# Another sequence of turns for a fused GLA-and-MLP kernel on one core

## The chip, the core and the metric

The kernel runs on one core of a Trainium2 chip. Five engines work side by side, each through its own instructions in its own fixed order: TensorE (PE; its weight loads are listed as PEld), VectorE (DVE), ScalarE (ACT), GpSimd (POOL) and SyncE (SP), which here issues nearly all DMA transfers. An engine that waits for a semaphore holds up everything that stands behind that instruction in its own order. The metric is the device time of one execution in microseconds (us), the median over several runs.

## The reference

Four batches, eight heads, 768 positions, head size 48. First a gated linear attention, a recurrence over the positions, then a layer norm, two matrix products with a relu between them, and a residual:

```python
for t in range(S):
    state = alpha[:, :, t, :, None] * state + np.einsum('bhd,bhe->bhde', k[:, :, t], v[:, :, t])
    y[:, :, t] = np.einsum('bhd,bhde->bhe', q[:, :, t], state)
...
xn = (x - mu) / np.sqrt(var + 1e-06) * g_ln
ch = np.maximum(xn @ w_ch1, 0.0) @ w_ch2
return (x + ch).astype(np.float32)
```

x is y with the heads side by side (4 x 768 x 384); w_ch1 is 384 x 1536 and w_ch2 is 1536 x 384.

## The kernel before, in words

The 768 positions are cut into six chunks of 128. An attention task is one chunk c of one batch b, so there are 24 of them, named by the letters a to x (letter number 4c + b). All tasks of one chunk feed one MLP stage, whose moving operand is the normalised x of all four batches, transposed (xT).

**Attention.** The task loads alpha, k, q and v; takes the logarithm of alpha (la, ACT, L341); sums it over the positions on PE (lps, L346 in chunk 0, L353 later); takes two exponentials (ACT, L356 and L357); multiplies them onto k and q (DVE, L359 and L361). q and k are then transposed: for tasks a to l on PE (tps, L413, copied out at L417, by ACT or DVE), for tasks m to x with a DVE transpose (L395) and a round trip through DRAM (four issues at L150 write "rows", four at L407 read qT and kT). PE makes the scores (aps, L426 or L441), DVE masks them into "at" (L450 or L455). PE makes the state updates (ups, L470); DVE adds the old state and POOL multiplies by the gate, twice from chunk 1 on (L483 and L485: mid, then st). The gate is a row of the exponentials that went through DRAM (written at L367, read at L461). PE makes y (yps, L496 or L506), ACT copies it to x (L515, L516, L518), x is saved to DRAM (kept, L530), the norm follows (L534 to L548). Its result is transposed by PE (xps, L564) or, from task i on, by DVE and a round trip through DRAM (L554, then "xrows" at L150, read at L559).

**MLP.** Chunk 0 is computed plainly (hps L589, ops L601, final add L605). Chunks 1 to 5 use sums of blocks prepared in advance, so that fewer products are needed: hps at L891 (15 products of two matmuls, twice per chunk) and ops at L713 (20 products of four matmuls per chunk). The results are put together by ACT (L903, L922, L930, L737), DVE (L907 to L920, L727, L730) and POOL (L905 to L918, L733).

**Weights.** They arrive as 64-bit numbers in eight pieces (ws, loaded at L238 into two staging buffers, 1,152 KB each), and DVE and ACT convert each piece: DVE at L250, L252 and L254, ACT at L256, DVE at L260 and then L263 (first matrix) or L266 (second). The block sums of the weights are made by DVE at L836 and L666, those of the activations at L861 and L695.

**What sets the order.** Every task is a Python generator which emits a few instructions and yields. One string, ORDER, names a generator per character; its order is the order in which all instructions are emitted, and so the order on every engine:

```python
turns = {"YZ"[h]: first_of_chunk_0(h) for h in range(2)}
turns |= {"PQ"[h]: second_of_chunk_0(h) for h in range(2)}
turns |= {chr(ord("a") + n): attention(n // B, n % B) for n in range(NCB * B)}
turns |= {chr(ord("A") + i): take_weights(i) for i in range(len(pieces))}
turns |= {"M": mlp(), "V": hidden_products(NCB - 1), "S": combine_first(), "W": combine_weights(), "R": relus(),
          "X": (x for c in range(1, NCB) for x in combine_x(c)),
          "N": (x for c in range(1, NCB) for x in combine_hidden(c)), "O": outputs()}
with tc.manual_schedule():
    for turn in ORDER:
        next(turns[turn], None)
```

Nothing moves an instruction afterwards. Waits come from data and from buffers that are used in turn: six PSUM banks (tag "bank"), eight row buffers ("row", which holds la, x, xn and xt), twelve "sum" buffers (qT, kT, block sums and the u of the MLP), six input buffers ("in"). Who gets a buffer after whom also follows from ORDER. SP's DMAs share eight landing semaphores in turn, so an issue can also wait until the eighth DMA before it has landed.

Of the kernel before, what the change touches and what calls it, by code (L numbers as in the profile page):

```python
# [25 lines left out]


ORDER = (
    "aaaacbdacaaabcdbbabcacaacbbbbaaabcdedcafbbcccdacbAaafebaceafcbcddcfefadebabefaAc"
    "ccfeffcdefdeedffffffffddeebBbbgbhgdgghAaiabAddbdbcddhhgddidfjggYYcccgYiYYAedefcg"  # L30
    "YgjdeefeechZeiZfhijfiihhBehjBiBZihBZZhhhhhhhhhYYlZZYCfZZgfCZgZejYYiCgYkfggjfjjjj"
    "YklDZjjjjjghjkjjghkhDiihhDZZZZjlfeCgeiiehDkfikYYYYkeYlkgllEllhYighEmZlligYYkkYjh"
    "ZSYinhYSlEljnEmihlllflOnllFFjikgkZZZlZjnZZjnjFhkjjemnjfnQkGkkfegilQfSSSkGfSSlFml"
    "gkmmmPihPjlngkkmmhGglPiHSghXniQHkPXXHSSSOXllPXllooWSPppoXoSlllQjnnlnnnnoonnpSmnn"
    "mmkXOXXommXPppjmipXQnWOpOSnoQomSpWkmOmQlmSnkWnmkQMMMMMMMMiMMkMMMMMnWMMMMWpllMMMM"
    "MPMMMMnrWnpppppppppqnoMWonMrpOGrqorWWWoMrrroooMkMMWrjMMMMMMMMMMRMmMMMMRMRMqpMMjq"
    "pMOjmRnpRMMMpMiqpRqRpoRqNMoMMMtMNNRpkMNiNMMMMMnqRNmmmNMoMMMMMNNMMNsjNNNMMrqMMMMn"
    "MMMMMMoorrrprrprWrrXMpXXXXqqqqtsMNMMMpotoMNMNMXXrqrXtptmXMMMMMMMMMMMMMXXtttsMnss"
    "MMMMMsqsqsMMpsMMOMMMMMMMqrrMMMMMMMooMMRMMMqMnrMMMMMMMMMMMrRRRMMMvMMMMttOtttuqtOr"
    "tttstossrRvpnsssRRRRNvuMMMNqMMMvRMrMstrOvuNmvvtqsvrrosrtNMNNNpNrNqMMMMMMMuNssMMs"  # L40
    "ssMuurNuuMMNMMMMNOXXXXXXXtMMtMXrMXMMMxwtMMMNMNNwxtttwwwXMtMwMMMMMsMMMMMMMtMMMXMM"
    "MMMMMMMMMMMMMMMuvtqttvvvvvvvrOwvOuvwxuvuxxxquuRMMMwMMMMMMMMMMMMMMRRRMMMMMMMMMMMM"
    "MvvvqxxxxusxxxxxxRxwwwxRRRRwwMuRuqsqMMNNNMMMuuutMuuuNxxMOuwxNNxvNwwwwsNNuvvvvNNN"
    "vNvtMMMMMMMMMMMvHMMMxMXXXXXXXXXMXMMMXMMxxxMMMMNNMMwwNMMvwwwxwxxMMMMMMMMMMMMMMMMM"
    "MMMMMMMMMMMMMMMMMMMMMMMMMMMMMMxORRMMMMMMRMMMMMMMMMMMROOxxXvRRRXRRRNMXXMMMXXMMXVO"
    "NXMMMNNNNNNNNNNNXXMVVMMMMXMVVVVVVVVVVVVVVVVVVVMVVVMMMMMMMVVVVVVVVVVVVVVVVVVVMMVV"
    "VVVVVVMMMMMMMVMVVNNVVVMRNRRRRRVRRMRMMVNNOMMMMMMOMRONNNNNMNMMMMNNNMMMMOMMMMMMMNMN"
    "MMMMNMMNNMMMMMMMMMMMMMM"
)


# [941 lines left out]
```

## Time and profile before

| | us |
|---|---|
| median of 3 runs | 419.85 |
| lowest and highest of them | 417.24, 420.99 |
| the profiled execution, its own time | 421.96 |
| its span, first to last instruction | 420.2 |
| start of its last instruction on an engine (DVE, L727) | 417.16 |

| engine | busy us | instructions |
|---|---|---|
| PE | 409.8 | 4616 |
| DVE | 294.8 | 554 |
| ACT | 217.4 | 522 |
| POOL | 119.7 | 134 |

The three runs differ among themselves by 3.75 us, and the profiled execution is 2.11 us over their median. A matrix product of 32-bit numbers shows as two PE records, so 4616 records are 2368 matmuls and transposes (a transpose is one record). The granted PE clock is full in all 40 slices of the page. DMA engines are busy 0.87 of the first 36 us, 0.84 of 36 to 106 us, 0.72 of 106 to 122 us and 0.60 of 147 to 337 us, and nearly idle after that. DVE is busy 64.4 of the 70 us between 36 and 106 us, and 122.0 of the 190 us between 147 and 337 us.

In what follows a time in us is on the axis of the profile. A "busy" PE need not be PE at its best, since its records overlap; what counts is the step from one matmul's start to the next one's.

### The profile page before, as it was taken

How to read it: one execution, taken by the hardware profiler on the slowest of the kernel's cores; microseconds unless marked ns; L12 is line 12 of the kernel's file. 1: busy time of each engine (PE TensorE's matmuls, PEld its weight loads, DVE VectorE, ACT ScalarE, POOL GpSimd, SP SyncE). 2: the span in 40 equal slices, each digit the busy share in tenths (PEclk: the TensorE clock that was granted, in tenths of full speed). 3: DMA queues.
4: the chain of work that ended last, by engine and by line, in shares of the span. 5: the costliest groups of instructions: out<-in, count | busy, mean ns of one | idle time of the engine just before them, and what ended most of it. 6: DMA issues, size and time to landing. Idle time of an engine off the chain costs nothing.

```text
span 420.2 us, 11451 instructions
## 1 busy us (share of the span) xinstructions
PE 409.8 (98%) x4616; PEld 354.9 (84%) x4616; DVE 294.8 (70%) x554; ACT 217.4 (52%) x522; POOL 119.7 (28%) x134
## 2 busy tenths in 40 slices
PE   7999999999999899999999999999999999999997
PEld 5877888876568689998889998889998889999996
DVE  3897999998988788688358973569534188215754
ACT  4797567783364378244576235864253643245110
POOL 1011013140011544124561253360135331525300
PEclk9999999999999999999999999999999999999999
DMA  8989978877778576955776858636423300000301
GB/s 269 280 234 262 285 168 275 239 171 202 224 151 210 156 150 150 209 136 115 176 152 145 209 158 212 106 62 113 133 56 113 76 1 2 19 0 21 112 20 57
DMA packets 134445, 61.26 MB, mean 146 GB/s; under 512 B 90956, under 2 KB 131276, under 8 KB 134392
## 3 DMA queue, kind: packets, MB, share of 16 engines
q1 hardware_dynamic: 133848, 60.37, 56.7%
q8 instruction: 36, 0.59, 0.6%
q10 hardware_dynamic: 544, 0.17, 0.2%
q14 instruction: 17, 0.14, 0.1%
HBM read 43.12 MB, written 17.39 MB: 144 GB/s over the span
## 4 chain that ended last, share of the span: by engine, by line
PE 78%; DVE 6%; DMA 5%; SPq 4%; ACT 3%; issue 2%; POOL 0%; DVEq 0%; ACTq 0%; POOLq 0%
PE ops L713 31%; PE hps L891 30%; PE hps L589 5%; PE yps L506 3%; PE ups L470 2%; PE aps L441 2%; SPq L150 1%; PE lps L353 1%; PE tps L413 1%; DMA rk<-in_k_dram 1%; DMA ws<-in_moe_w_ch_dram 1%; DMA kT<-rows 1%; PE aps L426 1%; SPq L407 1%; DMA xrows<-xt 1%
## 5 line engine op out<-in xcount | busy, mean ns | idle before, releaser
L891 PE MATMUL hps<-sum,w 128*128 128x256 f32 x192 | 46.3, 383 | 0.0
L713 PE MATMUL ops<-w,hT 128*128 128x192 f32 x224 | 40.8, 326 | 0.8 <-ACT hT L930 0.8
L891 PEld LDWEIGHTS hps<-sum,w 128*128 128x128 f32 x192 | 35.6, 190 | 6.3 <-ACT u L903 1.7
L737 ACT COPY u<-ops 128x192 f32<-128x192 f32 x30 | 9.5, 318 | 55.9 <-PE ops L713 55.8
L713 PEld LDWEIGHTS ops<-w,hT 128*128 128x128 f32 x224 | 37.2, 190 | 1.4 <-ACT hT L930 1.1
L733 POOL TENSOR_TENSOR ob<-ob,u 128x192 f32<-128x192 f32 x32 | 20.6, 656 | 57.8 <-ACT u L737 33.6
L485 POOL TENSOR_TENSOR mid<-mid,gate 112x192 f32<-112x192 f32 x20 | 12.3, 613 | 83.1 <-DMA gate<-row 45.8
L589 PE MATMUL hps<-xT,w 128*128 128x256 f32 x144 | 33.9, 385 | 0.5 <-DVE w L263 0.5
L903 ACT COPY u<-hps 128x512 f32<-128x512 f32 x32 | 18.7, 585 | 28.6 <-PE hps L891 22.7
L891 PE MATMUL hps<-xT,w 128*128 128x256 f32 x136 | 33.3, 379 | 0.0
L601 PE MATMUL ops<-w,hT 128*128 128x384 f32 x96 | 32.6, 491 | 0.0
L589 PEld LDWEIGHTS hps<-xT,w 128*128 128x128 f32 x144 | 26.2, 190 | 4.5 <-ACT few L537 0.7
L903 ACT COPY hT<-hps 128x512 f32<-128x512 f32 x40 | 23.3, 586 | 12.3 <-PE hps L891 12.1
L891 PEld LDWEIGHTS hps<-xT,w 128*128 128x128 f32 x136 | 25.8, 190 | 3.4
L713 PE MATMUL ops<-ws,sum 128*128 128x192 f32 x160 | 28.6, 327 | 0.0
L601 PEld LDWEIGHTS ops<-w,hT 128*128 128x128 f32 x96 | 17.7, 190 | 11.7 <-issue 0.6
L713 PEld LDWEIGHTS ops<-ws,sum 128*128 128x128 f32 x160 | 26.4, 190 | 0.7 <-ACT few L537 0.6
L727 DVE TENSOR_TENSOR ob<-ops,ob 128x192 f32<-128x192 f32 x40 | 13.1, 351 | 17.3 <-PE ops L713 10.8
L930 ACT ACTIVATE hT<-hT 128x512 f32<-128x512 f32 x40 | 22.9, 621 | 2.1 <-DVE hT L910 2.1
L713 PE MATMUL ops<-ws,hT 128*128 128x192 f32 x128 | 23.4, 326 | 0.0
L713 PE MATMUL ops<-more,sum 128*128 128x192 f32 x120 | 22.2, 328 | 0.0
L730 DVE TENSOR_TENSOR ob<-ob,ops 128x192 f32<-128x192 f32 x35 | 11.8, 348 | 13.9 <-PE ops L713 13.4
(223 smaller groups left out, 1041.3 us busy)
## 6 DMA issues: line engine op xcount, KB each, us to landing
ws<-in_moe_w_ch_dram SPq DMA_DIRECT2D x8, 1152.0 KB
vn<-in_v_dram SPq DMA_DIRECT2D x12, 384.0 KB
kept<-x SPq DMA_DIRECT2D x24, 192.0 KB
ob<-kept SPq DMA_DIRECT2D x24, 192.0 KB
rows<-rj SPq DMA_DIRECT2D x48, 96.0 KB
out_dram<-ob SPq DMA_DIRECT2D x18, 192.0 KB
xrows<-xt SPq DMA_DIRECT2D x64, 48.0 KB
xT<-xrows SPq DMA_DIRECT2D x16, 192.0 KB
```

The costliest lines, as they stand in the source:

```text
L485: nc.gpsimd.tensor_mul(new, new, by)
L506: nc.tensor.matmul(yps[j][halves[s], i, p], of, by, skip_group_check=True, start=not (cross and k), stop=k == 1 or not cross)
L589: nc.tensor.matmul(hps, w1[:, f, j * P:(j + 1) * P], xT_of[0][:, f, bs], start=(f == 0), stop=(f == NF - 1))
L601: nc.tensor.matmul(ops_of[b], hT_of[c][:, j, b], w2[:, j], start=(j == 0), stop=(j == NJ - 1))
L713: nc.tensor.matmul(acc, lhs[:, j], rhs[:, j], start=j == 0 and n not in FOLLOWS, stop=j == NT - 1 and n not in FOLLOWS.values(), skip_grou ...
L727: nc.vector.tensor_add(x, acc, x)
L730: nc.vector.tensor_sub(x, x, acc)
L733: getattr(nc.vector if c + 1 == NCB else nc.gpsimd, f"tensor_{op}")(x, x, y)
L737: copy(out=copied[n], in_=acc)
L891: nc.tensor.matmul(acc[:, i], w, b, start=n not in JOINS and i == 0, stop=n not in JOINS.values(), skip_group_check=True)
L903: nc.scalar.copy(out=copied[n], in_=acc)
L930: nc.scalar.activation(out=x, in_=x, func=AFT.Relu)
```

## The change

ORDER is another string with the same characters, each as often as before, so every generator makes the same steps in the same order, and only their interleaving differs. Instructions, shapes, buffers and engines are the same; in the built programs each engine has the same instructions of every kind, 2368 matmuls and transposes on PE, 432 DMA issues on SP and so on.

```diff
--- before.py
+++ after.py
@@ -26,26 +26,26 @@
 
 
 ORDER = (
-    "aaaacbdacaaabcdbbabcacaacbbbbaaabcdedcafbbcccdacbAaafebaceafcbcddcfefadebabefaAc"
-    "ccfeffcdefdeedffffffffddeebBbbgbhgdgghAaiabAddbdbcddhhgddidfjggYYcccgYiYYAedefcg"
-    "YgjdeefeechZeiZfhijfiihhBehjBiBZihBZZhhhhhhhhhYYlZZYCfZZgfCZgZejYYiCgYkfggjfjjjj"
-    "YklDZjjjjjghjkjjghkhDiihhDZZZZjlfeCgeiiehDkfikYYYYkeYlkgllEllhYighEmZlligYYkkYjh"
-    "ZSYinhYSlEljnEmihlllflOnllFFjikgkZZZlZjnZZjnjFhkjjemnjfnQkGkkfegilQfSSSkGfSSlFml"
-    "gkmmmPihPjlngkkmmhGglPiHSghXniQHkPXXHSSSOXllPXllooWSPppoXoSlllQjnnlnnnnoonnpSmnn"
-    "mmkXOXXommXPppjmipXQnWOpOSnoQomSpWkmOmQlmSnkWnmkQMMMMMMMMiMMkMMMMMnWMMMMWpllMMMM"
-    "MPMMMMnrWnpppppppppqnoMWonMrpOGrqorWWWoMrrroooMkMMWrjMMMMMMMMMMRMmMMMMRMRMqpMMjq"
-    "pMOjmRnpRMMMpMiqpRqRpoRqNMoMMMtMNNRpkMNiNMMMMMnqRNmmmNMoMMMMMNNMMNsjNNNMMrqMMMMn"
-    "MMMMMMoorrrprrprWrrXMpXXXXqqqqtsMNMMMpotoMNMNMXXrqrXtptmXMMMMMMMMMMMMMXXtttsMnss"
-    "MMMMMsqsqsMMpsMMOMMMMMMMqrrMMMMMMMooMMRMMMqMnrMMMMMMMMMMMrRRRMMMvMMMMttOtttuqtOr"
-    "tttstossrRvpnsssRRRRNvuMMMNqMMMvRMrMstrOvuNmvvtqsvrrosrtNMNNNpNrNqMMMMMMMuNssMMs"
-    "ssMuurNuuMMNMMMMNOXXXXXXXtMMtMXrMXMMMxwtMMMNMNNwxtttwwwXMtMwMMMMMsMMMMMMMtMMMXMM"
-    "MMMMMMMMMMMMMMMuvtqttvvvvvvvrOwvOuvwxuvuxxxquuRMMMwMMMMMMMMMMMMMMRRRMMMMMMMMMMMM"
-    "MvvvqxxxxusxxxxxxRxwwwxRRRRwwMuRuqsqMMNNNMMMuuutMuuuNxxMOuwxNNxvNwwwwsNNuvvvvNNN"
-    "vNvtMMMMMMMMMMMvHMMMxMXXXXXXXXXMXMMMXMMxxxMMMMNNMMwwNMMvwwwxwxxMMMMMMMMMMMMMMMMM"
-    "MMMMMMMMMMMMMMMMMMMMMMMMMMMMMMxORRMMMMMMRMMMMMMMMMMMROOxxXvRRRXRRRNMXXMMMXXMMXVO"
-    "NXMMMNNNNNNNNNNNXXMVVMMMMXMVVVVVVVVVVVVVVVVVVVMVVVMMMMMMMVVVVVVVVVVVVVVVVVVVMMVV"
-    "VVVVVVMMMMMMMVMVVNNVVVMRNRRRRRVRRMRMMVNNOMMMMMMOMRONNNNNMNMMMMNNNMMMMOMMMMMMMNMN"
-    "MMMMNMMNNMMMMMMMMMMMMMM"
+    "aaaaaaaabccbccdbbbddaaabbccbbdbaaaaaebcccccfdfecAbebaaaaeeecccabdfddadaaefdebbbc"
+    "fccccfeeffffdAhfgdffdfffffedgebbabbgAbBigAdgadbbdfgghdhhigdiYYdAYfeiddYggeYccdce"
+    "jeiecYidieehfeefihBchchhhfBZZBZZZhhhjjjhhBehhhghifZZfZZjgeeelihCYYYfYglgkkCCjZYf"
+    "kZgkYDjjYjYYgjgjjjjjjjjjYhhZZhDZZgZiilfhfDgCiklDZYfhlhiYkgiikZElkkkhlfEYlFYjmYee"
+    "ElYYniYimnjjlllSliiihlllESFfSjjllZjZZglZZkkggngikgFZjnjnQhkgknQglihkkjilkGPhmSFm"
+    "kGkkOkkmklPGnmhmnmhnlfmlQfhlHlSSkHillHWXWplPlXXPPSSSooopQXXXOoPXSXnSnnnnnnplljnm"
+    "mOmnnmomjlQSSoppmmoQpWpPoPQmmXSSnSSMMMMWMWjWXXOMMWWWnnMMMMMMMmnMMOMMMnMMMjMMMpMo"
+    "ninrpMMmlMMMQpnpppppqMppoRoqmpiRjrrHrooOrkpjnrOkoOWMMMMMqWMMMMMMMMMMjoMMMMpqMpMn"
+    "pMMMMRMrqqioRRRRoRqlooRNRpppMoMkMNNMNNqMMMMMNNmpNomMMMMWMMMMMMMnNNNNMrqtrNmmMMMM"
+    "MMMMWMmsMprrrrrrrrMXXXXtsqqqpssMNNMOoNMooMptMrXXXMssssnMXMXXoXMMMqrstMMMMMMMMMpM"
+    "ttqqqMMMMMOnpMMMMMMtMMMMtqrqqqOpMqrquMrMMMMMMMMMMMMMMMMRMMvMrrMMMMMMMMMMMttmttOt"
+    "RttRRRtRRRtoRtsssssstvvuuvMMMvpMvnpvMnqsstsoNNuuuuRrrrrrNNMMMMNMMuMMvMNMNMsNMNNM"
+    "MNNsMMMMtNXXXXMMXXXXXXrrMMMMMMMMMMwrtutNttqxMNwtxtwsMMMNwOMwtXMMMOMMwMMMMwMMsMvM"
+    "MMMMMMtMMMMMMMMMMvvwvvvvvvvvMuuuutxOxrOxuxsRMMMMMMMMMMwssMMMMMMMMMMMMMMMMMMxtRMM"
+    "vvRRuRxxxxxxxxxxRRRxwwwtRwxtMMMMqMvuNwsuuuMuMqxvNwuvNMRxNNMNNNMMMwMMMMMMMuNvNqrN"
+    "sNNMMtMuMMMMMMXXXXXxXwwwwwwXXMMMxxMXXMNxOxuNNuxvMMMMMxMwwXMMMMMxMMMxMMMMvMvvvvxv"
+    "MMMMMMMMMMMMMMMMMMMMMOMMMMMMMOMMGMMMMMMMMMRRRMxRMMMMMMMMMRRwXXRXXXXXXXRMNXONNNMM"
+    "MMMMMMNNNMRRXMMVVVNNVVVVNNNNVMVVVVVVVVVVVVVVVMMVVVVVMVVVVVVMMMVVVVVVMVRVMRMMMMMM"
+    "OVVVVVVVRVVRVVMVVVVMMMMVVNMMRNMMRRRMRVNRNNNNMMMMMMMNNNNNNNOOOMNNMMMMMMMMMMNMMMMM"
+    "MMMMMMMMNNMMMMMMMMMMMMM"
 )
```

What it moves, by the built programs' instruction orders (the places that are spoken of below):

- **ACT, first tasks.** Before: la of a, b and c, the exponentials of a, la of d, the exponentials of b, then of d, the two first qT copies, then the exponentials of c. After: la of a, the exponentials of a, la of b, c and d, the exponentials of b, of d and of c, then the two first qT copies, b's ahead of a's.
- **DVE, weight pieces two and three.** Before, x (L521) and qk (L359) stand between L254 and L260 of piece two, and st, at (L455), and qk between those of piece three. After, nothing stands between them in piece two, and one mid (L483) in piece three.
- **SP, weight piece eight.** Before, its load (L238) stands behind a v load, four vx loads, the four "rows" issues of one of tasks m and n, and a gate; after, directly behind the vx loads and ahead of all "rows".
- **DVE, mid and st of task m.** Before, three instructions stand between mid (L483) and st (L483): L861, L359, L361. After, eight: L361, L534, L554, L836 twice, L395, L359, L361.
- **PE, around the ups of task n.** Before: ups of m, eight matmuls of L601, ups of n. After: ups of m, twelve matmuls of L601, the 32 matmuls of m's yps, ups of n.
- **DVE, weight sums.** Before, four of the thirteen L666 sums stand ahead of the first L912 of chunk 1; after, nine.
- **SP, scores of o and p.** The qT and kT issues of both tasks stand behind each other, after the loads of the next tasks' q and k. The last kT issues take over a "sum" buffer from the MLP's u, and so wait for POOL's first L905; before, they took one from a task's transposed q or k and waited for PE's yps. On PE, 2.1 us more work stands ahead of these scores.
- **ACT, the second la of chunk 4.** Before, it took a row buffer that four "xrows" DMAs were still reading; after, one whose last reader is a DVE transpose (L554). It now stands behind the L922 of chunk 1's first half; before, ahead of it.

## The prediction

> **What bounds the kernel now.** I read the page first, for the share of each engine, then the chain of waits in order of time, then PE's waits and DVE's.
>
> ```profile
> PE 409.8 (98%) x4616; PEld 354.9 (84%) x4616; DVE 294.8 (70%) x554; ACT 217.4 (52%) x522; POOL 119.7 (28%) x134
> PE 78%; DVE 6%; DMA 5%; SPq 4%; ACT 3%; issue 2%; POOL 0%; DVEq 0%; ACTq 0%; POOLq 0%
> ...
> 190.43 12.16 PE hps L891 x56
> 387.17 29.97 PE ops L713 x184
> ```
>
> The first line says that PE is all but full; the second, that 78% of the chain is PE. The last two give its pace: 12.16 / 56 = 0.217 us for each L891 record, 29.97 / 184 = 0.163 us for each L713 record. Summed from start-to-start steps of such rows: L891 600 x 0.216 = 129.6; L713 800 x 0.163 = 130.4; L589 144 x 0.216 = 31.1; L601 96 x 0.323 = 31.0; the attention's small matmuls 72; 63 changes between the full-array matmuls and others at 0.1, 6.3. That is 400.4 us which no order can save. The span is 420.2, so about 20 us are head, waits and tail: 3.1 us follow the last matmul, and the lag of PE behind its own summed work is 3.4 us when it has passed its first scores, 8.4 at 44 us, still 8.6 at 114 us, 12.5 at 145 us and about 16 at 340 us (of the last 3.6, 0.95 is one wait, the rest small drifts at changes of shape). So the order decides over little: the stretch up to 44 us, and 114 to 145 us.
>
> The single waits of PE that lie later than 100 us (engine, line waited for, then us in total, times, longest):
>
> ```profile
> PE ops L713 <- ACT hT L930: 0.8, 1, 0.8
> PE ups L470 <- DVE st L483: 0.7, 1, 0.7
> ...
> PE lps L353 <- ACT la L341: 0.5, 1, 0.5
> ...
> PE aps L441 <- DMA kT<-rows: 0.5, 1, 0.5
> ```
>
> and, from the engines' timelines, what stood behind them (the bracket is idle time and who ended it):
>
> ```profile
> 101.49 0.76 DVE L250 TENSOR_SCALAR w<-ws 128x1152 int32<-128x1152 int32 x1 [1.34 <-DMA ws<-in_moe_w_ch_dram]
> ...
> 122.33 0.36 DVE L483 TENSOR_TENSOR st<-ups,mid 112x192 f32<-112x192 f32 x1 [1.39 <-POOL mid L485]
> ...
> 121.79 0.51 POOL L485 TENSOR_TENSOR mid<-mid,gate 112x192 f32<-112x192 f32 x1 [21.05 <-DMA gate<-row]
> ...
> 137.57 0.99 SPq L407 DMA_DIRECT2D kT<-rows  x2
> ...
> 144.26 0.52 ACT L341 ACTIVATE la<-ra 128x384 f32<-128x384 f32 x1 [3.16 <-DMA xrows<-xt]
> ```
>
> A late transfer ends each: the gate held POOL's mid, that held DVE's st, and that held PE's ups; kT held the scores; the xrows DMAs held the row buffer that la needed, and la held PE's lps.
>
> **The change part by part.** Instructions, buffers and engines are the same, so PE's 400.4 us stay; the new order has 65 changes of shape instead of 63: +0.2.
>
> *Wait of ups at 122 us.* Start to start it cost 0.8 (idle 0.7 in the list). Before, 0.42 + 0.55 + 0.55 of DVE work (L861, L359, L361) lie between mid and st. After, L361, L534, L554, two L836, L395, L359 and L361: 0.55 + 0.20 + 0.56 + 2 x 0.69 + 0.97 + 0.55 + 0.55 = 4.8 us, which hide the gate's 2.4 us flight and POOL's 0.51; and four more L601 matmuls (8 x 0.323 = 2.6) and a yps (1.0) stand ahead of this ups on PE. -0.8; what is late next is the L912 below.
>
> *Wait of the scores at 140 us.* Two steps of 0.64 and 0.14 over their normal: 0.8. After, 2.1 us more PE work stands ahead. SP needs 18 issues from the second "rows" to the last kT instead of 19, so it is as late as before by its own pace (about 138 us), and with the 2.4 us from the last kT issue to the restart of PE kT lands at about 140.5; the scores are due at 132.2 (summed work) + 8.6 = 140.8 or later. But the last kT issues now wait for POOL's L905, which comes behind a mid of 0.51 and lasts 1.27, and that mid behind DVE's. With DVE's lag of 4 to 6.5 us at 129.3 us of its summed work, L905 ends between 135.3 and 137.8, kT lands between 138.6 and 141.1. -0.8, with ends -0.8 and +0.3. Rows on both sides exist for POOL: L485 took 0.51 to 2.02, and L666 on DVE 0.95 alone but 1.98 at 140 us, beside POOL's L917 and L918. I take the short end, because the instructions beside POOL's are then L912 and L920, with PSUM inputs. The Trainium skill ("SBUF — State Buffer", section "Who interferes with whom") says that a VectorE instruction with two SBUF inputs and a GpSimd one that reads SBUF exclude each other for their whole length, which fits these rows; with the long end, 1.5 more on POOL, the sum below would be 1 us higher.
>
> *Wait of lps at 144 us.* 0.69 and 0.16 over normal: 0.85. The new row buffer waits for no DMA, only for L554. But la now stands behind L922, which waits for PE: the product ends at about 131.2 + 8.6 = 139.8, L922 lasts 0.58 and la 0.52, so la is done at 141.0, and lps is due at 133.1 + 8.6 = 141.7. -0.85 (ends -1.3, with the la before it, and 0).
>
> *The head.* Three pairs of exponentials (0.49 each, 0.4 apart) instead of two now stand ahead of the first qT copies, and a's copy is second: the first scores start at about 12.5 instead of 11.7. Against that, DVE does L359 and L361 of the next chunk's first task where it idled 1.06 (19 us), and mid no longer stands so early that it waits 0.82 for ups (37.75 us). PE's first L589 waits for DVE's L263, with the same 26 us of DVE work ahead in both. 0, ends -2 and +0.8.
>
> *Weight pieces two and three.* From the end of L254 to the start of L260 lies ACT's L256 (1.37). Before, 1.0 and 2.5 us of DVE work hid it (idle 0.49 once); after, 0 and 0.35: about 1.0 and 1.1 us more DVE idle. PE needs piece two's L263 at 40.8 us of its work and DVE has it at 40.1 of its own, with a lag of about 8.5 there: 0 to 0.5 us of wait. Piece three is due 1.8 us of work later: none. +0.3; what goes further is the third rival.
>
> *Piece eight.* Its load leaves 3 us earlier (89.7 instead of 92.89), so the 1.34 us of DVE idle go. PE did not wait for it: 0. At 340 us the seam (L713 waits for L930) is as it was: 0.
>
> *DVE ahead of the first L912.* Nine L666 sums instead of four make it 130.0 us of DVE work, before 127.4, for matmuls due at 126.5 of PE's. PE lags 8.6, so DVE may lag 5.1; before, it was at 5.1 at 131.8 us with two idles of 1.34 and 1.39 in it that go. 0, ends 0 and +1.5.
>
> Sum: 0.2 - 0.8 - 0.8 - 0.85 + 0 + 0.3 = -1.95, so 421.96 - 2.0 = 420.0 for an execution like the profiled one. That one is 2.1 over the median, and 419.85 - 2.0 = **417.9**.
>
> **The rivals.** *The early lag goes too.* PE's lag grows by 5.0 between 9 and 44 us. If DVE paces it there, the 1.06, 0.82 and 0.37 of idle that go take 2.2 more: 415.7, and with all ends (la 0.45, early waits 0.5) 414.5. For: L589 waits for L263. Against: the weights' arrival (23.85 us) does not move.
>
> *Slower: DVE carries the uncovered L256 into the MLP.* The place is L912 at 126.5 us of PE work. If nothing absorbs the 2.1 us of new idle and the 2.6 us of sums put ahead, less the 2.7 that go, DVE is 2 us later there than PE can stand; L905, kT and la follow it, and the three savings are lost: 419.85 + 2.0 + 0.5 = 422.4, up to 425 with POOL's long end. It decides when DVE's lag at its 130.0 is over 5.1. For: DVE is busy 92% from 36 to 106 us. Against: before, its lag fell from 8.8 at 62 us to 5.3 at 119.
>
> *No change.* The same late transfers reach other instructions: 419.9. For: SP issues as many in the same stretch.
>
> **How the numbers follow.** Forecast 0.47 (416 to 419.5), early lag 0.20, slower 0.25, no change 0.08. A measurement of this kernel can tell about 1%, 4.2 us: 415.65 and 424.05. Faster by more: most of the early-lag case and the forecast's far edge, 0.22. Slower by more: a good half of the slower case, 0.15. Within: 0.63. The range reaches from 413.8 to 423.8, the early-lag case with its ends and the slower one without its last piece.
>
> **What would show it.** Right: no wait of ups on st, no scores on kT, no lps on la over 0.2 us between 114 and 150 us; no L250 idle near 98 us; two L260 idles of about 1.4 near 45 and 54 us. Wrong: an L891 that waits for L912 or L836 near 135 us, SP's kT issue after 138 us on POOL, a longer wait up to 44 us, or a median over 419.85.

## The result, and the profile after

| | before | changed |
|---|---|---|
| median of 21 runs each | 419.75 us | 421.22 us |
| lowest and highest | 417.24, 423.95 | 420.52, 424.93 |
| ratio of times, 95% interval | | 1.0044 [1.0022, 1.0065] |
| profiled execution, its own time and span | 421.96, 420.2 | 424.93, 423.1 |

The changed order is slower by 0.44%, some 1.8 us. A second comparison gave 1.0064 [1.0039, 1.0089]. The forecast was 2.0 us faster. Seven of the 21 executions of the kernel before took over 420.5 us, and all 21 of the changed one did: the shortest of the two lie 3.3 us apart, the medians 1.5. The lines of the page that stood ahead of the prediction, for the changed kernel:

```profile
PE 409.5 (97%) x4616; PEld 354.0 (84%) x4616; DVE 294.3 (70%) x554; ACT 215.3 (51%) x522; POOL 119.6 (28%) x134
...
PE 88%; DVE 5%; ACT 2%; issue 2%; DMA 1%; SPq 0%; DVEq 0%
```

Busy times are the same to 1%, and the chain has hardly any DMA or SP pieces (5% and 4% before). That is what the forecast wanted, but it is not the work of the change: a second profile of the kernel before, from the next section, has none to speak of either:

```profile
PE 94%; ACT 3%; DMA 1%; DVE 0%; issue 0%; SPq 0%; DVEq 0%
```

In the changed kernel, PE's waits (engine, line waited for, then us in total, times, longest) tell where the time went instead:

```profile
PE yps L506 <- issue: 3.5, 2, 2.1
PE hps L589 <- DVE w L263: 1.6, 2, 0.9
PE lps L346 <- ACT la L341: 1.4, 1, 1.4
PE aps L426 <- ACT qT L417: 1.2, 1, 1.2
...
PE ops L713 <- ACT hT L930: 0.8, 1, 0.8
PE ups L470 <- DVE st L483: 0.5, 1, 0.5
PE tps L413 <- DVE qk L361: 0.4, 1, 0.4
```

The three late waits of before (on st near 122 us, kT near 140, la near 144) are not there. New or longer are four: on qT near 12 us, on L263 near 33 and near 49 us (before, one of 0.5), and on st near 64 us. (The wait on la near 7 us, L346, varies: between nothing and 1.8 us in the profiles with the head in the order before, 1.4 in all six with the changed one.) The 3.5 us of L506 have no releaser, and the next section shows that they belong to this one execution.

Weight piece eight looks as forecast. Of the 1.34 us of idle ahead of its L250 nothing is left (timeline of DVE; a bracket would show idle time):

```profile
105.80 0.73 DVE L250 TENSOR_SCALAR w<-ws 128x1152 int32<-128x1152 int32 x1
```

But the second profile of the kernel before has no idle there either, so this was not the change's doing:

```profile
99.17 0.75 DVE L250 TENSOR_SCALAR w<-ws 128x1152 int32<-128x1152 int32 x1
```

### The profile page after: what moved, and what is told of

It is laid out like the page before. It is cut to its first block, busy times and chain, and to the rows that moved or that the text cites. A ratio compares the mean times of both kernels' runs of the same rounds, so it can differ in the third digit from the quotient of the medians.

```text
span 423.1 us, 11445 instructions
## 1 busy us (share of the span) xinstructions
PE 409.5 (97%) x4616; PEld 354.0 (84%) x4616; DVE 294.3 (70%) x554; ACT 215.3 (51%) x522; POOL 119.6 (28%) x134
## 4 chain that ended last, share of the span: by engine, by line
PE 88%; DVE 5%; ACT 2%; issue 2%; DMA 1%; SPq 0%; DVEq 0%
PE hps L891 31%; PE ops L713 31%; PE ops L601 8%; PE yps L506 5%; PE hps L589 4%; PE ups L470 2%; PE aps L441 2%; PE tps L413 2%; DMA rq<-in_q_dram 1%; PE lps L353 1%; PE aps L426 1%; DVE w L252 1%; ACT ws L256 1%; DVE w L250 1%; PE yps L496 1%
## 5 line engine op out<-in xcount | busy, mean ns | idle before, releaser
L733 POOL TENSOR_TENSOR ob<-ob,u 128x192 f32<-128x192 f32 x32 | 22.1, 700 | 66.2 <-ACT u L737 26.6
L485 POOL TENSOR_TENSOR mid<-mid,gate 112x192 f32<-112x192 f32 x20 | 13.7, 685 | 87.3 <-DVE mid L483 38.6
L589 PE MATMUL hps<-xT,w 128*128 128x256 f32 x144 | 34.1, 386 | 1.6 <-DVE w L263 1.6
L601 PE MATMUL ops<-w,hT 128*128 128x384 f32 x96 | 32.6, 491 | 0.0
L589 PEld LDWEIGHTS hps<-xT,w 128*128 128x128 f32 x144 | 25.9, 190 | 7.3 <-ACT lps L357 1.6
L891 PEld LDWEIGHTS hps<-xT,w 128*128 128x128 f32 x136 | 25.6, 190 | 3.4
L601 PEld LDWEIGHTS ops<-w,hT 128*128 128x128 f32 x96 | 17.7, 190 | 11.7 <-issue 0.6
L506 PE MATMUL yps<-mid,qT 48*64 48x48 f32 x320 | 20.5, 221 | 2.1 <-issue 2.1
```

The source lines that it names most:

```text
L485: nc.gpsimd.tensor_mul(new, new, by)
L506: nc.tensor.matmul(yps[j][halves[s], i, p], of, by, skip_group_check=True, start=not (cross and k), stop=k == 1 or not cross)
L589: nc.tensor.matmul(hps, w1[:, f, j * P:(j + 1) * P], xT_of[0][:, f, bs], start=(f == 0), stop=(f == NF - 1))
L601: nc.tensor.matmul(ops_of[b], hT_of[c][:, j, b], w2[:, j], start=(j == 0), stop=(j == NJ - 1))
L733: getattr(nc.vector if c + 1 == NCB else nc.gpsimd, f"tensor_{op}")(x, x, y)
L891: nc.tensor.matmul(acc[:, i], w, b, start=n not in JOINS and i == 0, stop=n not in JOINS.values(), skip_group_check=True)
```

## The experiments

Two measures are used. The ratio is to the kernel before on the same chip in the same comparison. The lag is the one of the prediction: when a matmul starts, less PE's summed work ahead of it; its growth over a stretch is what PE lost there. The lag is of one execution. The intervals reach 0.2 to 0.4% (0.7 to 1.6 us) to each side, and the changed kernel itself gave 1.0044 and 1.0064 in two comparisons, so the ratios alone do not settle a single step of about 1 us. Kernels made of two orders take the first n turns of one, and then all turns that are left in the sequence of the other.

| kernel | ratio, 95% interval | lag at 8 | 25.6 | 41 | 62 | 100 | 134 | 323 us of PE work |
|---|---|---|---|---|---|---|---|---|
| before, first profile | | 3.7 | 7.1 | 8.1 | 8.4 | 8.3 | 12.5 | 16.2 |
| before_again | 1.0007 [0.9977, 1.0036] | 3.8 | 6.7 | 7.4 | 7.8 | 7.7 | 8.6 | 12.1 |
| after_again | 1.0064 [1.0039, 1.0089] | 4.6 | 7.6 | 9.2 | 10.2 | 10.1 | 10.7 | 14.7 |
| head_before_rest_after | 1.0015 [0.9988, 1.0041] | 4.5 | 7.3 | 8.2 | 8.6 | 9.0 | 9.5 | 14.1 |
| head_after_rest_before | 1.0086 [1.0058, 1.0115] | 4.6 | 8.0 | 9.6 | 10.6 | 10.6 | 12.8 | 16.4 |
| head_restored | 1.0028 [1.0002, 1.0054] | 3.8 | 7.3 | 8.8 | 9.8 | 9.8 | 10.4 | 14.4 |
| cover_restored | 1.0030 [1.0010, 1.0049] | 4.6 | 7.5 | 8.1 | 8.8 | 8.8 | 9.4 | 13.4 |
| head_and_cover | 1.0012 [0.9994, 1.0031] | 3.6 | 7.1 | 7.7 | 8.2 | 8.7 | 9.0 | 13.2 |
| three_restored | 0.9989 [0.9967, 1.0010] | 3.5 | 5.9 | 6.4 | 7.0 | 6.9 | 7.5 | 11.6 |
| three_and_old_tail | 0.9982 [0.9965, 0.9999] | 3.3 | 5.7 | 6.3 | 7.1 | 7.1 | 7.7 | 11.3 |

**Both kernels once more.** No edit.

> The kernel before once more, for a second profile. Three theories on the result: (early) the changed order loses time in every execution ahead of 72 us, at the first scores, at the waits for L263 near 33 and 49 us and at an ups near 64 us, and gains about 2 us at the three late waits (122, 140, 144 us); (issue) the two stalls of L506 with no releaser, 3.5 us together near 70 and 76 us, belong to the changed order and come in every execution; (luck) the three late waits of the kernel before were 2.3 us in its one profile but are mostly absent from its typical execution, so that removing them gains little. Here: early, the three waits are there again with 1.5 us or more together; luck, under 0.8 us together, and in both the ratio is 1.000 within its interval.

> The changed kernel once more, for a second profile. Issue: L506 waits for nothing shown for 3 us or more again. Early and luck: under 1 us of that; PE's lag behind its summed work is then about 10.5 us at the place of the second stall, and the waits for qT near 12 us (1.2), for L263 near 33 and 49 us (0.9 and 0.7) and for st near 64 us (0.5) are all there again. Ratio 1.002 to 1.007 by all three.

PE's waits, first of the kernel before:

```profile
PE lps L286 <- DVE more L283: 1.1, 1, 1.1
PE ops L713 <- ACT hT L930: 0.8, 1, 0.8
PE aps L426 <- ACT qT L417: 0.6, 2, 0.4
PE lps L346 <- ACT la L341: 0.5, 1, 0.5
PE tps L413 <- DVE qk L359: 0.4, 1, 0.4
PE hps L589 <- ACT few L537: 0.2, 1, 0.2
PE hps L589 <- PE aps L441: 0.2, 1, 0.2
```

then of the changed one:

```profile
PE hps L589 <- DVE w L263: 1.6, 2, 0.9
...
PE aps L426 <- ACT qT L417: 1.2, 1, 1.2
...
PE ups L470 <- DVE st L483: 0.6, 1, 0.6
```

The same program of before, in another execution, has none of the three late waits: this one's own time is 417.92 us, the first one's was 421.96. Between 100 and 134 us of PE work the lag grew by 4.2 in the first and by 0.9 here. In the changed kernel, the early waits came back to within a tenth and the L506 stalls did not; its own time is 420.72. So the theory of "issue" falls. Of "early", the part on the early losses stands, and its 1.5 us or more at the late waits is a miss here, where "luck" holds. What differed in the kernel before is when SP got to the last kT issue of that stretch. In the timeline of SP it is now

```profile
133.94 0.99 SPq L407 DMA_DIRECT2D kT<-rows  x2
```

and was at 137.57 in the first profile. There SP's own waits for landed transfers between 110 and 145 us summed to more: 3.4 us against 1.5 for xrows, and 1.5 against none for loads of q and k.

**The order cut at 62 us of PE work.**

```diff
-ORDER = AFTER
+ORDER = BEFORE[:305] + rest of AFTER      # head_before_rest_after
+ORDER = AFTER[:305] + rest of BEFORE      # head_after_rest_before
```

> The first 305 turns of the kernel before (PE work up to 62 us), then all that is left in the changed order. Early: the early losses go and the three late waits stay away, 417 to 418.5 us, ratio 0.993 to 0.998. Issue: the stall near 76 us stays, the one near 70 may; about 420, ratio 1.000. Luck: 419 to 420, ratio 0.998 to 1.001.

> The first 305 turns of the changed kernel, then all that is left in the order before. Early: both costs, the early losses and the three late waits, 422.5 to 424 us, ratio 1.007 to 1.010. Issue: at most one of the two stalls, about 421. Luck: as slow as the changed kernel, 421 to 422, ratio 1.003 to 1.006.

With the early part as before, 419.06 us (the kernel before: 418.58 in the same comparison), a miss for "early", which wanted 418.5 or less, and as "luck" has it. With only the early part changed, 422.15 us: between the two ranges in us, and with its ratio of 1.0086 inside that of "early". So most of the loss lies in the first 62 us of PE work, where the lag of the changed kernel is 10.2 and that of the kernel before 7.8 and 8.4. The part behind, in which the three waits were to be saved, gains nothing that shows; the intervals leave room for a loss there too (see the tail, below).

**Which places of the early part.** Head, and the cover of weight piece two:

```diff
-ORDER = AFTER
+ORDER = BEFORE[:93] + rest of AFTER       # head_restored
+ORDER = AFTER[:92] + rest of BEFORE       # new_head_alone
...
-YidieehfeefihBchc
+YidieehfihBeefchc                         # cover_restored, turns 165 to 181 of AFTER
```

In the second edit "B" is the turn with L250, L252 and L254 of piece two; the turns "e" (x, L521) and "f" (mid, L483) move behind it. head_and_cover has both edits.

> The changed kernel with its first 93 turns (PE work up to 19 us, all before the first weight piece is converted) in the order before. Theory of additive terms: the wait for qT falls from 1.28 to 0.3 us and that for L263 at 33 us from 1.05 to 0.35; PE's lag at its first L589 falls from 7.6 to 6.7 and the kernel by about 0.9, to 420.7 us where the changed one gives 421.7; ratio to before 1.003 to 1.005. Theory of one pacer: VectorE sets the stretch up to the L263 of piece two, near 48 us, so whatever the head gains waits there; under 0.4 us gained, ratio 1.005 to 1.007.

> The changed kernel with two DVE instructions (x at L521, mid at L483) put between L254 and L260 of weight piece two, where the kernel before had two; nothing else moves. Additive: the idle ahead of that L260 falls from 1.43 us to 0.6 or less, L263 of piece two comes 0.8 to 1.3 us earlier, PE's wait for it near 49 us (0.78) goes, and the kernel is 0.8 faster than the changed one, about 420.9, ratio 1.004 to 1.006. One pacer, with the wait turning up again at the ups near 64 us: that wait grows from 0.67 to over 1.2 and the time stays at 421.5 or more.

> Both of these. Additive: 1.7 us less than the changed kernel, 420.0, ratio 1.001 to 1.004, with the ups near 64 us as the only wait left of those that the change brought. One pacer: both are needed and either alone gives little, so 420 too, but the two single ones stay over 421.4. If the ups near 64 us takes all back: 421 or more.

> The kernel before with only its first 92 turns in the changed order. Additive: the first scores wait 1.28 us for qT, the first L589 waits 1.05, and the kernel is 0.9 us slower than before, ratio 1.002 to 1.0035. One pacer: the slack of the later DVE work, whose cover is there, takes it up; under 0.4 us, ratio 0.999 to 1.001.

Head restored: the wait for qT fell from 1.28 to 0.28 us (start to start over the normal step) and the ratio went from 1.0064 to 1.0028; but the wait of the first L589 stayed at 1.07, where 0.35 was expected. The new head alone on the kernel before gave 1.0022 [0.9991, 1.0052], with the wait for qT at 1.28 and that of L589 at 0.31. So the wait for qT is the head's, and the first L589 is another matter. What the head costs is less than the 0.8 us by which the lag at 8 us differs. With the head restored the first scores start at 11.78 us instead of 12.62, 0.84 earlier; the first L589 at 33.16 instead of 33.52, 0.36 earlier; the span is 418.6 instead of 418.9. More than half was taken up on the way, as "one pacer" has it, and 0.3 to 0.4 us stayed; the ratios, of two comparisons, would give 1.5 us. (The lag at 8 us also varies by itself: head_before_rest_after has 4.5 with the head in the order before.)

Next the cover. The timeline of DVE around piece two in the kernel before (second profile):

```profile
40.48 1.35 DVE L250 TENSOR_SCALAR w<-ws 128x1152 int32<-128x1152 int32 x1
...
43.25 0.76 DVE L254 TENSOR_SCALAR ws<-ws 128x1152 int32<-128x1152 int32 x1
43.93 0.55 DVE L521 SCALAR_TENSOR_TENSOR x<-yps,x 128x384 f32<-128x384 f32 x1
...
44.40 0.55 DVE L359 TENSOR_TENSOR qk<-rk,lps 128x384 f32<-128x384 f32 x1
45.45 1.36 DVE L260 SCALAR_TENSOR_TENSOR ws<-ws 128x1152 int32<-128x1152 int32 x1 [0.50 <-ACT ws L256]
46.84 1.80 DVE L263 SCALAR_TENSOR_TENSOR w<-w,small,ws 128x384 f32<-128x384 f32 x3
```

in the changed kernel (second profile):

```profile
41.28 0.56 DVE L521 SCALAR_TENSOR_TENSOR x<-yps,x 128x384 f32<-128x384 f32 x1 [0.47 <-ACT x L518]
...
41.76 0.35 DVE L483 TENSOR_TENSOR mid<-ups,st 112x192 f32<-112x192 f32 x1
42.03 1.34 DVE L250 TENSOR_SCALAR w<-ws 128x1152 int32<-128x1152 int32 x1
...
46.99 1.36 DVE L260 SCALAR_TENSOR_TENSOR ws<-ws 128x1152 int32<-128x1152 int32 x1 [1.43 <-ACT ws L256]
48.38 1.80 DVE L263 SCALAR_TENSOR_TENSOR w<-w,small,ws 128x384 f32<-128x384 f32 x3
```

and with the cover restored:

```profile
40.62 1.34 DVE L250 TENSOR_SCALAR w<-ws 128x1152 int32<-128x1152 int32 x1
...
45.57 1.36 DVE L260 SCALAR_TENSOR_TENSOR ws<-ws 128x1152 int32<-128x1152 int32 x1 [0.68 <-ACT ws L256]
46.97 1.80 DVE L263 SCALAR_TENSOR_TENSOR w<-w,small,ws 128x384 f32<-128x384 f32 x3
```

From the start of L250 to that of L263 it is 6.36, 6.35 and 6.35 us in the three: while ACT does L256 there is a slot of some 1.4 us, and what fills it costs nothing. What stands ahead of L250 instead pushes the whole conversion back. In the changed kernel that is x with its own 0.47 us of waiting for ACT, and mid: 0.47 + 0.48 + 0.27, about 1.2 us from start to start, and L263 came 1.41 us earlier when they were moved. PE's wait near 49 us (0.78) went, and the span fell from 418.9 to 417.6. The ratio is 1.0030, and with the head 1.0012: the cover alone gains, against "one pacer", which wanted both single ones to stay slow. The ups near 64 us did not take it back (wait 0.67, then 0.57 and 0.38).

**The same cover taken from the kernel before.**

```diff
-iihhBehjBiBZ
+iihhejBhBiBZ                              # turns 180 to 191 of BEFORE
```

> The kernel before with x (L521) and qk (L359) moved ahead of weight piece two, so that nothing stands between its L254 and L260. Additive: the idle ahead of that L260 grows from 0.50 to about 1.4, its L263 comes 0.9 later, PE's second group of L589 waits for it 0.5 to 0.9, and the kernel is that much slower: ratio 1.001 to 1.0025. Rival, the recorded price: DVE's lag leaves room there, 0 to 0.3 us, ratio under 1.0008.

424.66 us, ratio 1.0136 [1.0097, 1.0174], over five times what was expected: a miss for both. DVE's timeline shows why this is no clean mirror:

```profile
42.42 0.56 DVE L521 SCALAR_TENSOR_TENSOR x<-yps,x 128x384 f32<-128x384 f32 x1 [0.63 <-ACT x L518]
...
44.57 0.55 DVE L359 TENSOR_TENSOR qk<-rk,lps 128x384 f32<-128x384 f32 x1 [1.58 <-ACT lps L357]
45.04 1.34 DVE L250 TENSOR_SCALAR w<-ws 128x1152 int32<-128x1152 int32 x1
...
49.94 1.36 DVE L260 SCALAR_TENSOR_TENSOR ws<-ws 128x1152 int32<-128x1152 int32 x1 [1.37 <-ACT ws L256]
```

The idle ahead of L260 is the 1.4 us that were expected, but the two moved instructions wait for ACT, 0.63 and 1.58 us, and now L250 waits behind them: it starts at 45.04 instead of 40.48. On ACT the L256 that waits for L254 stands ahead of the next qT and kT copies, and PE's scores wait 2.5 us for them. Then comes a second loss: right behind that stop the granted PE clock, 1.00 before and after, is 0.50 for 3.41 us. First the matmuls behind the stop, then the stretch itself (its length; busy us and instructions of PE, PEld, DVE, ACT and POOL; granted clock; DMA share; GB/s):

```profile
50.92 1.75 PE L441 MATMUL aps<-qT,kT 48*64 48x64 f32 x60 [2.52 <-ACT qT L417]
...
51.23:54.64 3.41, 3.41 (x61) 2.93 (x53) 3.38 (x6) 0.00 (x0) 0.44 (x1) 0.50 0.53 144
```

At half the clock 3.41 us do 1.7 us of work, so some 1.7 us are lost there, an estimate. The mean clock was 0.992 to 0.996 in five of the six executions, which took 424.22 us or more, and 0.999 in the sixth, which took 422.55. So of the 5.7 us that the ratio stands for, about 2.5 are the stop and 1.7 the clock; the rest was not traced. That the stop lowered the clock is read from the order of events. No such stretch lies between 11 us and the last matmul in any other profile here, nor behind the two stops of 1.45 and 2.06 us in the first profile of the changed kernel.

**The first L589 and ACT's order.** In the changed kernel ACT's L256 of piece one starts at 29.43 (28.47 before), because the exponentials of task g, which wait for PE's lps, stand ahead of it; DVE's L260 is idle 0.72 for it. One turn is moved:

```diff
-gebbabbgAbBigA
+gebbabbAgbBigA                            # turns 108 to 121 of AFTER; three_restored, piece_one_alone
...
-bbgbhgdgghAaia
+bbgbhgdAgghaia                            # turns 108 to 121 of BEFORE; before_piece_one
```

> The kernel with head and cover restored, and ACT's L256 of weight piece one put ahead of the two exponentials of task g, behind which it waited for PE's lps. Additive: that L256 starts 1 us or more earlier, the wait of the first L589 for L263 (1.07) falls under 0.3 us, and the kernel gains 0.7: ratio to before 0.9985 to 1.0005. Rival: the exponentials that are put off hold the qk of task g and so its tps; the gain is under 0.3, ratio 1.0005 to 1.002.

> The changed kernel with one turn moved: ACT's L256 of weight piece one goes ahead of the two exponentials of task g, which wait for PE's lps. Nothing of the head or of piece two is restored. If the third cost (the wait of 1.07 us of the first L589 for L263, which stayed with the head restored) is this queueing on ACT: L256 starts about 1.2 us earlier, that wait falls to 0.3 or less, L250 of piece two comes about 1 us earlier too, and the kernel gains 0.7 to 1.2, ratio to before 1.003 to 1.005. If it is the late head after all: under 0.4 gained, ratio 1.0055 or more.

> The same turn moved in the kernel before, where L260 of piece one has no idle ahead of it. If the gain comes only from the idle ahead of L260: under 0.4 us, ratio 0.999 to 1.001. If ACT's order decides there too (its first L589 waits 0.34 us): 0.4 to 0.8 us faster, ratio 0.998 to 0.999.

With head and cover also restored, L256 starts at 26.91, L260 has no idle, the first L589 waits 0.70 instead of 1.07, and the ratio is 0.9989 [0.9967, 1.0010]. The time is in the range of "additive", with the span down from 417.4 (head_and_cover) to 415.8; the wait is not, as 0.3 or less was expected, and PE's list puts what is left of it down to ACT's L356, no longer to L263. Alone the move gave 420.4 us, ratio 1.0054 [1.0037, 1.0071], no more than 0.4 us, a miss. DVE's timeline shows what took the place of the idle ahead of L260:

```profile
30.54 0.56 DVE L359 TENSOR_TENSOR qk<-rk,lps 128x384 f32<-128x384 f32 x1 [1.35 <-ACT lps L357]
31.02 1.35 DVE L260 SCALAR_TENSOR_TENSOR ws<-ws 128x1152 int32<-128x1152 int32 x1
```

The qk of task g stands ahead of L260 and now waits 1.35 us for the exponentials that were put off. With the head late, ACT came to L256 at 28.33 only, and to the exponentials at 29.66; in three_restored they start at 28.25. In the kernel before it gave 1.0010 [0.9994, 1.0026], nothing, as the theory of the idle ahead of L260 has it.

**The late stretch and the tail alone.**

```diff
-ORDER = BEFORE
+ORDER = BEFORE[:470] + rest of AFTER up to turn 717 + rest of BEFORE   # late_alone
+ORDER = BEFORE[:716] + rest of AFTER                                   # tail_alone
+ORDER = THREE_RESTORED[:716] + rest of BEFORE                          # three_and_old_tail
```

> The kernel before with only its stretch from 106 to 159 us of PE work (the one with the three late waits) in the changed order. In the four profiles so far with this stretch in the order before, the late waits took 2.4, 0, 0.5 and 0.9 us, 0.96 in the mean. Theory of luck: their removal gains about that mean, 0.3 to 1.0 us in the median, ratio 0.9975 to 0.9995, no late wait in the profile, and the slow executions of before (over 420.5 us) become rarer. Rival, the recorded forecast's price: 2 us or more, ratio under 0.996. Second rival: the stretch costs elsewhere what it saves, ratio 1.000 or more.

> The kernel before with only what follows 159 us of PE work in the changed order. PE's lag grew by 4.0 to 4.5 us from 134 to 323 us of PE work in the profiles with this part in the changed order and by 3.5 to 3.9 with it in the order before. Theory that the tail costs too: 0.3 to 0.7 us slower than before, ratio 1.0005 to 1.002. Rival: the difference belongs to single executions; ratio 0.999 to 1.0005.

> The kernel with the three early places restored, and all that follows 159 us of PE work in the order before. If the changed tail costs what its run alone showed (ratio 1.003, 0.8 to 1.3 us): 417.2 to 417.8 us where three_restored gave 418.5, ratio 0.9955 to 0.9975, faster than both kernels. If that run showed single executions: 418.5, ratio 0.998 to 1.000.

late_alone: 419.70 us, ratio 1.0008 [0.9984, 1.0032]. The 2 us of the forecast are outside the interval. Its profile still has a wait for kT (0.90), so this mixture is no clean test of the saving. SP's own waits between 110 and 145 us show what held SP:

```profile
SPq L367 <- ACT lps L357: 4.5, 1, 4.5
```

In the mixture one task's exponentials stand behind the norm work on ACT (L538 to L548) and end at 121.85 us, and SP stands at the write of their row until then, with "rows" and kT behind it. In three_restored all of these exponentials stand ahead of that norm work (the last starts at 112.17), and neither that wait of SP nor one of PE for kT is there. No run moved this alone. tail_alone: 1.0030 [1.0008, 1.0053]; but taking the old tail in three_restored changed 0.9989 into 0.9982 only. That the changed tail costs something is likely, 0.3 to 1.3 us; how much stays open. three_and_old_tail is a little faster than the kernel before, 417.24 us against 417.79 in the same comparison, ratio 0.9982 [0.9965, 0.9999]; the interval just excludes 1, and it is one of sixteen, so this is weak.

## Why the prediction was wrong

- **What bounds it:** right in the main. PE's summed work did not change, and the early stretch decides most. But the sum has no term for the order behind 159 us of PE work, and the runs put 0.3 to 1.3 us there.
- **The three late waits:** the mechanism was right, the size was not. None is in either profile of the changed kernel, nor in the seven others with that stretch in its order, late_alone apart. But their 0.8 + 0.8 + 0.85 us were one execution's. In the first four profiles with this stretch in the order before they took 2.4, 0, 0.5 and 0.9 us, and no run shows more than some 0.8 us of gain from their removal (three_and_old_tail, if that is its cause). The step that failed is the last of the sum: "That one is 2.1 over the median, and 419.85 - 2.0". The 2.1 us by which that execution was over the median are about these waits, and the forecast took them off the median once more.
- **The head:** priced at 0. The later start was forecast to the tenth (0.8 us: 12.62 against 11.81 in the second profiles). It was assumed to be absorbed, since DVE has as much work ahead, and more than half of it was: 0.3 to 0.4 us stayed.
- **Weight pieces two and three:** priced at +0.3. The new idle was sized well for piece two (0.50 to 1.43), less so for piece three (0.81, forecast 1.4). The wait of PE was put at 0 to 0.5 and was 0.78, since L263 had no slack to lose, and restoring the cover alone gave 1.3 us by the spans. What the step overlooked is where the covering work went: ahead of L250, with x's wait.
- **Piece one:** priced at 0 with the head, because PE's first L589 waits for L263 "with the same 26 us of DVE work ahead in both". That step counted DVE's work and not DVE's wait inside it: L260 was idle 0.72 us for ACT's L256. In both orders that stands behind the exponentials of task g, and these waited for PE until 28.63 us, where it was 27.67 in the kernel before. Putting L256 ahead gave 1.6 us by the spans with head and cover restored (417.4 to 415.8), and 0.5 alone.
- **Zero terms that held:** piece eight (its idle was gone in the kernel before too, in the second profile); the seam near 340 us (0.8 in every list); no wait at the first L912. POOL took the short end: L485 0.51 and L905 1.27 us, beside L912 and L920. In the kernel before, second profile, L666 beside L917 took 1.99.
- **The rivals:** the slower one gave nearly the time (422.4), but for the wrong place. It wanted the uncovered L256 to come out at L912; it came out at once, at the next L589. The rival that the early lag goes too is answered by the lag at 41 us of PE work, 9.2 against 7.4: it grew.

Made again from the second profiles, the lag differs by 0.8 at 8 us of PE work, 0.9 at 25.6, 1.8 at 41, 2.4 at 62 and at 100, 2.1 at 134 and 2.6 at 323. The spans differ by 418.9 - 416.1 = 2.8. The forecast for such a pair of executions, without late waits to save, would have been 0.2 + 0 + 0.3 = 0.5: what it lacked are the two weight pieces, the rest of the head and the tail.

## What to carry to other kernels

A wait that is seen in one profile of an execution above the median may be part of that excess; before its removal is priced, profile the kernel again, and take only what both show off the median. The same holds for a wait that is gone afterwards: see first whether a second profile of the kernel before has it. An idle slot that another engine's step leaves in an in-order queue is free room: work moved from it to the place ahead of that step costs its whole length, and its own waits too. When two starts are compared by "the same work ahead", count the waits inside that work too: here DVE waited for ACT, and ACT for PE.

## What was not expected of the hardware

In the first profile of the changed kernel PE stopped twice in the middle of L506, near 69.2 and 75.4 us, with no semaphore to wait for. The trace has 36 transfers of 16,384 bytes in a queue for instructions (the page of the profile: "q8 instruction: 36, 0.59"). That is one for each 256 of PE's 9,232 records of matmuls and weight loads, so they are read as PE's. Two of them fit the stops:

```
instruction transfer   took     PE has started   PE goes on at
68.35                  0.98     1896 records     70.63
75.03                  1.02     2203 records     77.47
```

In the second profile the same two transfers started at 64.26 and 69.50 us, with 1811 and 2067 records started, and PE did not stop. The Trainium skill ("Runtime: NRT & Kernel Launch", section "Instruction fetch mechanics") says that instructions come in blocks of 16 KiB, 256 each, and that this is mostly hidden. The size agrees. Here it was not always hidden: 128 matmul records of L506 take 2.0 us (chain of before: "159.05 2.01 PE yps L506 x128") and are 256 records with their weight loads, so a block is soon used up; transfers that start 4.1 and 5.5 us later go with 3.5 us of standing still. That the transfer is the cause is read from the order of events; no run moved it alone.
